# Second products by seven half-size products in all twelve pairs, and a new list of single steps

## The chip, the cores and the metric

The kernel runs on one core of a Trainium2 chip. Its engines are TensorE (PE in the profile, with PEld for its weight loads), the vector engine (DVE), the scalar engine (ACT), GpSimd (POOL, which also issues most of the loads) and SyncE (SP, which issues the stores and the turned tiles). Each takes its own instructions in order, and they wait for each other on semaphores. The metric is the device time of one execution in microseconds. The kernel before takes 168.75 us (median of three runs, 168.35 to 170.79).

## The reference

Two stages. The first is a linear attention with a decaying state, over batch 4, 8 heads, 768 steps, 48 numbers a head:

```
for t in range(S):
    cur = einsum('bhd,bhe->bhde', u * k[t], v[t])
    y[t] = einsum('bhd,bhde->bhe', r[t], state + cur)
    state = w[:, None] * state + einsum('bhd,bhe->bhde', k[t], v[t])
```

The second takes y as 3072 tokens of 384 numbers through two matrices with a leaky gate between, 384 to 2048 and back to 384:

```
h = x @ w_in
g = maximum(0.01 * h, h)
out = g @ w_out
```

Inputs and output are 32-bit floats; the kernel multiplies in bf16 and adds in 32 bits.

## The kernel before

**Chunks and pairs.** The 3072 tokens are 24 chunks of 128 (six for each batch entry). A chunk n goes through these steps, named by the letter that they have in the list ORDER: loads of k, r and v (L213); P scales r and k by powers of the decay (L313); T turns the scaled tile with TensorE for chunks 0 to 7 (L369, evicted by L376), and from chunk 8 on P itself issues a turning DMA on SP (L316); A multiplies keys by queries into two PSUM banks (L389); M masks the scores into the tile `at` (L399 for chunks from 6 on, L407, L423 and L419 before); K multiplies keys by values (L439); S brings the state on (L482 and L484); Q computes the bonus of the same step, for chunks from 6 on by two products and a sum (L343, L345, L347), after which GpSimd writes it on the diagonal of `at` (L355), and the mask fills in the rest; Y multiplies scores by values and state by queries (L512) and is evicted to `xT` (L532).

Two chunks make a pair m of 256 tokens. G (a chunk and a quarter of the hidden units, L545) or J (a pair and an eighth, L562) is the first product of the second stage, evicted through the gate to `gT` (L550, L568). G serves pairs 0 and 1, J the others.

**The second product** has two forms. H takes a chunk: 16 matmuls of 384 columns into one bank (L579), one eviction (L585), a store. Z takes a pair in seven half-size products, the scheme of Strassen and Winograd: the pair's block of 256 tokens by 2048 hidden units is cut into 2 x 2 blocks, `w_out` too. V forms four sums of blocks of `w_out` once (`tw`, L599); B forms four sums of blocks of `gT` for each pair (`gs`, L617); each of seven products is eight matmuls of 192 columns (L651) into one of three banks, with part sums kept by ACT (`snap`, L659) and added by the vector engine (L682). H serves pairs 0 to 7, Z pairs 8 to 11.

**What sets the order.** ORDER is a written list. Each step records its operations, matmuls and evictions together, one engine after another; `Sched` keeps for every tile who wrote and who read it last, and from that puts the waits on each engine's stream. PSUM banks are dealt out in turn by `next_bank`, and `I` in the list skips some. The condition under which an earlier operation on the same engine isn't waited for stands in `Sched.add`:

```
if d.dma is None and d.eng == eng and dma is None and (eng == "pe" or not raw):
    continue
```

so an engine other than TensorE waits for its own earlier operation where it reads what that wrote, and not where it overwrites what that wrote or read.

Of the kernel before, what the change touches and what calls it, by code (L numbers as in the profile page):

```python
# [12 lines left out]
L = 128  # L13
# [10 lines left out]
EARLY = 3  # L24
ORDER = """
v0 U k1 k2 I1 P0 r1 P1.1 r2 k3 T0 F4 C W A0 r3 X0 P2.1 wi3 T1 K0 M0.0 Q0 T2 X1 S0 P3.1 Y0 X2 A2 M2.4 T3 v1 K1 G0.3 k4 Q1 A1 r4 A3 S1 P4 v2 K2 M1.2 T4 v3 k5 Y1 X3 Q2 M3.0 wi2 S2 K3 Y2 Q3 G1.3 G1.2 r5 r6 k6 v4 wi1 G2.2 v5 r7 wi0 v6 Y3 r9 k7 X4 P5 T5 k9 v7 S3 G2.3 P6 T6 Q6 G3.3 K4 A4 X5 G2.1 G0.1 Q4 K5 G1.1 G0.2 M4.4 Q5 A5 S4 M5.2 wo0 wo1 wo2 wo3 A6 Y4 G0.0 G3.1 Y5 M6 P7 G3.2 k8 r8 T7 G3.0 k18 Q7 K6 v10 r12 J2.3 r20 k13 J2.7 v8 r13 r11 S6 k10 J2.2 v20 k11 K7 G1.0 S7 G2.0 J2.6 A7 J2.0 Q9 P9 J2.5 J2.1 M7 J2.4 P8 H1 k12 r21 v9 I4 H0 H2 Y7 Y6 A9 Q8 I1 A8 v21 H3 J3.3 K8 M9 H4 M8 S8 J3.4 J3.7 v13 k20 k14 r10 J3.6 v12 Q13 k16 Y8 k23 Y9 r15 r14 H5 J4.0 J4.3 J3.5 v14 Q11 v23 k15 K9 P12 J4.4 J4.7 J4.5 J4.2 P11 P10 J3.0 I3 Q12 J3.2 P13 I1 S9 P14 K10 J4.6 J4.1 K12 Q10 S10 K13 S12 J3.1 H8 A12 r17 S13 v11 k17 v16 r18 P15 I1 A10 H9 M12 A11 M10 A13 H6 Q15 M11 K14 M13 Y10 I1 v17 k21 Y11 v19 Y12 S14 Y13 P17 r19 Q14 A15 v15 A14 J5.3 v22 J5.7 r16 J5.5 H7 Q17 v18 M15 I4 M14 J5.1 J5.2 J6.4 J6.1 J6.7 J6.2 J6.0 Y14 Q18 I1 P18 Y15 k22 r22 k19 A17 r23 J5.0 K15 J7.5 J7.3 J5.4 S15 P16 I4 J6.3 K16 J6.6 K18 M17 J6.5 Q16 J7.2 P21 S16 J7.0 A18 S18 M18 P19 H13 I1 J7.7 Q20 P20 I2 J5.6 Q21 J7.1 J7.4 K19 J7.6 K20 S19 H10 H12 H11 S20 A20 Q19 A19 A16 H14 M20 H15 M19 M16 A21 Y16 Y17 Y18 I1 V0 V1 M21 Y20 Y19 Y21 J8.1 Q23 J8.0 P23 K21 J8.7 J9.5 P22 S21 J8.6 J9.4 J9.7 K22 J8.5 V2 J8.3 Q22 I2 J9.1 S22 J8.2 J9.2 J8.4 A22 M22 A23 B8.0 M23 B8.2 B8.1 J10.0 J9.3 B8.3 J10.7 J9.6 V3 Z8.0 Y23 Y22 J9.0 B9.0 B9.2 J10.1 B9.1 J10.2 J10.6 I4 Z8.1 J10.3 Z8.2 B9.3 Z8.3 J11.2 Z8.4 Z8.5 I2 J10.5 Z8.6 J10.4 J11.4 B10.2 J11.0 J11.3 J11.6 J11.5 Z9.0 J11.1 Z9.1 B10.0 J11.7 Z9.2 B11.0 Z9.3 Z11.0 Z10.0 B11.1 Z9.4 Z10.1 B11.2 Z9.5 Z9.6 I1 B10.1 Z11.1 Z11.2 B11.3 Z10.2 Z10.3 B10.3 Z11.3 Z11.4 Z11.5 Z10.4 Z11.6 Z10.5 Z10.6
# [7 lines left out]
class Sched:  # L34
# [8 lines left out]
    def add(self, eng, emit, R=(), W=(), dma=None):  # L43
# [73 lines left out]
def bass_rwkv5_eagle__then__act_leaky_relu_kernel(  # L117
# [68 lines left out]
    taken = [0]  # L186

    def next_bank():
        i = taken[0] % 8
        taken[0] += 1  # L190
        return ps[i], ("ps", i)

    def dram(h, offset, pattern):
        return bass.AP(tensor=h.tensor, offset=h.offset + offset, ap=pattern)

# [8 lines left out]
    def load_one(n, which, pace=()):  # L204
# [8 lines left out]
        add("pool", lambda: G.dma_start(dst, src), R=pace, W=[key], dma=f"{which}{n}")  # L213

    def load_two(n, which, pace=()):
        load_one(n, which, pace)
        load_one(n + 1, which, pace)

    def load_pair(n, pace=()):
        for i in (n, n + 1):  # L220
            for which in "krv":
                load_one(i, which, pace)
# [11 lines left out]

    def row(h):
        return dram(h, 0, [[HD, 1], [1, HD]])

    add("sp", lambda: SP.dma_start(w_row[:, :], row(w)), W=["w_row"], dma="w")
    add("act", lambda: A.dma_start(u_row[:, :], row(u)), W=["u_row"], dma="u")
    load_first("r")  # L240
    load_first("k")
    for hh in range(2):
        for name, src, dst in (("wcol", w, wcol), ("ucol", u, ucol)):
            add("sp", lambda src=src, dst=dst, hh=hh: SP.dma_start(
                dst[64 * hh:64 * hh + D, :], dram(src, hh * D, [[1, D], [2 * D, NP], [1, 1]]), allow_slow_non_contiguous=True),
                W=[f"{name}{hh}"], dma=f"{name}{hh}")
    add("act", lambda: A.preload_act_table_set("natural_log_exp_and_others"))
    add("pool", lambda: G.iota(ramp[:, :], pattern=[[1, 128]], base=0, channel_multiplier=-1,  # L248
                               allow_small_or_imprecise_dtypes=True), W=["ramp"])
    add("dve", lambda: V.memset(ones[:, :], 1.0), W=["ones"])  # L250
    add("dve", lambda: V.memset(one_row[:, :], 1.0), W=["one_row"])
    add("dve", lambda: V.memset(one_row16[:, :], 1.0), W=["one_row16"])

    def fill(n):
        i = taken[0] % 8

        def emit():
            for _ in range(n):
                last = PE.matmul(ps[i][:, :], ones[:, 0:128], ones[:, :], start=True, stop=True)
            return last  # L260

        add("pe", emit, R=["ones"], W=[("ps", i), f"fill{n}"])

    def skip(n):
        taken[0] += n

    ps_w, key_w = next_bank()

    def load(name):
        if name[:2] == "wi":  # L270
            load_win(int(name[2:]))
        elif name[:2] == "wo":
            load_wout(int(name[2:]))
        elif name[:2] in ("rr", "kk", "vv"):
            load_two(int(name[2:]), name[0])
        else:
            load_one(int(name[1:]), name[0])

    add("dve", lambda: V.tensor_scalar(kexp[:, :], ramp[:, 0:1], 1.0, float(MID - 1), ALU.mult, ALU.add),
        R=["ramp"], W=["kexp"])  # L280
    add("dve", lambda: V.tensor_scalar(qexp[:, :], ramp[:, 0:1], -1.0, float(-MID), ALU.mult, ALU.add),
        R=["ramp"], W=["qexp"])
    add("dve", lambda: V.tensor_scalar(ident[:, :], ramp[:, :], 0.0, None, ALU.is_equal), R=["ramp"], W=["ident"])
    add("dve", lambda: V.memset(v_sb[:, :, :].rearrange("p n (h e) -> p (n h) e", e=E)[:, :, D:E], 0.0), W=["v0"])
    add("dve", lambda: V.tensor_scalar(mask[:, :], ramp[:, :], 1.0, None, ALU.is_ge), R=["ramp"], W=["mask"])
    for i in range(NQK):
        add("dve", lambda i=i: V.memset(qk[i][:, :, D:E], 0.0), W=[("qk0", i)])
    add("dve", lambda: V.memset(wl[:, :, :], 0.0), W=["wl"])
    add("dve", lambda: V.memset(wu[:, :, :], 0.0), W=["wu"])
    add("act", lambda: A.activation(u_row16[:, :], u_row[:, :], AF.Copy), R=["u_row"], W=["u_row16"])  # L290
    fill(EARLY)
    add("pe", lambda: PE.matmul(ps_w[:, 0:HD], one_row[:, :], w_row[:, :], start=True, stop=True),
        R=["one_row", "w_row"], W=[key_w, "bc"])
    add("act", lambda: A.activation(lnw[:, :], ps_w[:, 0:HD], AF.Ln), R=[key_w], W=["lnw"])
    add("act", lambda: A.activation(qtab[:, :], lnw[:, :], AF.Exp, scale=qexp[:, 0:1]), R=["lnw", "qexp"], W=["qtab"])
    add("act", lambda: A.activation(ktab[:, :], lnw[:, :], AF.Exp, scale=kexp[:, 0:1]), R=["lnw", "kexp"], W=["ktab"])
    at_bank, kv_bank, turns = {}, {}, {"sum": 0, "s": 0}

    def hd(x):
        return x.rearrange("p (h d) -> p h d", d=D)  # L300

    def k_of(n):
        return k_sb[:, n % NRK, :] if n else k0_f[:, :]

    def r_of(n):
        return r_sb[:, n % NRK, :] if n else r0_f[:, :]

    def prep(n, how=0):
        iq = n % NQK
        if n >= 4 or how:  # L310
# [495 lines left out]
```

## Time and profile before

| | us |
|---|---|
| median of the runs | 168.75 |
| the profiled execution | 170.19 |
| its span, first to last instruction | 168.4 |
| TensorE busy | 158.4 (94%) |
| vector engine busy | 112.5 (67%) |
| ACT busy | 94.1 (56%) |
| GpSimd busy | 88.4 (52%) |

A row of the chain of waits gives start, length and the work that the end depended on. A row of a stretch gives its bounds, its length, busy time (and instructions) of PE, PEld, DVE, ACT and POOL, the granted clock (1.00 is full), the share of the DMA engines and GB/s. A row of a group gives line, engine, operation, tiles out<-in with shapes, how many; then busy us and mean ns of one; then the idle time of the engine just before them and what ended it. A timeline row gives start, length and the instruction. A matmul's length there contains its latency; how fast matmuls follow each other is read from the chain.

### The profile page before, as it was taken

Reading aid. Unit: us, or ns where it says so; the run is one execution under the profiler, and the core shown is the slowest. Engines: PE = TensorE matmul, PEld = TensorE weight load, DVE = VectorE, ACT = ScalarE, POOL = GpSimd, SP = SyncE. Lnnn points to the kernel's source line nnn. Section 1 sums busy time; section 2 is a strip of 40 time slices with the busy share of each in tenths; the row PEclk is TensorE's granted clock in tenths of the full one; section 3 lists DMA queues with packets and bytes.
Section 4 is the critical chain, followed back from the end, with each engine's and each line's share of the span. In section 5 each row is a group of like instructions: output and inputs, shape, how many; then the busy total and the mean of one; then the engine's idle time right before and its main releaser. Section 6 shows DMA issues by size and latency. Waiting matters only on the chain.

```text
span 168.4 us, 5024 instructions
## 1 busy us (share of the span) xinstructions
PE 158.4 (94%) x2166; PEld 125.5 (75%) x2166; DVE 112.5 (67%) x205; ACT 94.1 (56%) x179; POOL 88.4 (52%) x101
## 2 busy tenths in 40 slices
PE   6677897999999999999999999999999999999993
PEld 2245796898666778965778886766698889999992
DVE  7398989938405678759896399924899396313571
ACT  4765586787413366841548783521288788385310
POOL 7999999679999199581988732320032000000000
DMA  5999999999999999999999985512126000110224
GB/s 98 120 140 149 166 183 159 194 202 146 139 137 187 178 157 136 183 163 174 129 156 165 128 97 106 125 47 96 48 64 115 0 4 0 47 51 0 77 69 140
DMA packets 100090, 19.67 MB, mean 117 GB/s; under 512 B 93154, under 2 KB 100068, under 8 KB 100068
## 3 DMA queue, kind: packets, MB, share of 16 engines
q0 software_dynamic: 76512, 10.03, 94.2%
q1 hardware_dynamic: 22514, 9.12, 26.2%
q8 instruction: 17, 0.28, 0.7%
q10 hardware_dynamic: 1042, 0.20, 0.6%
q14 instruction: 5, 0.04, 0.1%
HBM read 20.45 MB, written 4.72 MB: 149 GB/s over the span
## 4 chain that ended last, share of the span: by engine, by line
PE 82%; POOL 10%; DMA 6%; issue 1%; ACT 0%; POOLq 0%; ACTq 0%
PE ps_all L562 31%; PE ps_all L579 25%; PE ps_all L651 11%; POOL rk_sb L213 6%; DMA w_in_sb<-in_moe_w_in_dram 6%; PE ps_all L512 5%; PE ps_all L545 4%; PE ps_all L389 3%; POOL v_sb L213 3%; PE ps_all L439 2%; POOL w_in_sb L228 1%; PE ps_all L517 0%; PE ps_all L369 0%; ACT out_sb L675 0%; POOL ramp L248 0%
## 5 line engine op out<-in xcount | busy, mean ns | idle before, releaser
L562 PE MATMUL ps_all<-xT,w_in_sb 128*128 128x256 bf16 x480 | 57.0, 273 | 0.0
L568 ACT ACTIVATE gT<-ps_all 128x512 bf16<-128x512 f32 x80 | 47.8, 597 | 12.3 <-PE ps_all L562 8.7
L562 PEld LDWEIGHTS ps_all<-xT,w_in_sb 128*128 128x128 bf16 x480 | 45.8, 98 | 6.1
L579 PE MATMUL ps_all<-w_out_sb,gT 128*128 128x384 bf16 x256 | 43.5, 326 | 0.0
L355 POOL TENSOR_SCALAR_AFFINE_SELECT at<-s_tok 128x1024 bf16<-128x1024 f32 x18 | 21.0, 1168 | 40.9 <-DVE s_tok L347 40.9
L579 PEld LDWEIGHTS ps_all<-w_out_sb,gT 128*128 128x128 bf16 x256 | 24.4, 98 | 15.8
L399 DVE CAST_PREDICATED at<-mask,ps_all 128x1024 bf16<-128x1024 uint16 x18 | 21.4, 1219 | 18.6 <-PE ps_all L389 18.5
L585 ACT ACTIVATE out_sb<-ps_all 128x384 f32<-128x384 f32 x16 | 7.9, 492 | 37.0 <-PE ps_all L579 37.0
L213 POOL DMA_DIRECT2D v_sb<-in_v_dram x24 | 22.6, 946 | 0.3 <-issue 0.3
L213 POOL DMA_DIRECT2D rk_sb<-in_k_dram x23 | 21.3, 937 | 0.0
L213 POOL DMA_DIRECT2D rk_sb<-in_r_dram x23 | 21.2, 930 | 0.0
L313 DVE TENSOR_TENSOR qk<-rk_sb,tab 128x768 bf16<-128x768 bf16 x23 | 14.5, 638 | 3.9 <-DMA rk_sb<-in_r_dram 3.7
L545 PE MATMUL ps_all<-xT,w_in_sb 128*128 128x128 bf16 x192 | 12.5, 219 | 1.6 <-DMA w_in_sb<-in_moe_w_in_dram 1.1
L482 DVE TENSOR_TENSOR sum_t<-ps_all,st 128x384 bf16<-128x384 f32 x14 | 7.8, 554 | 9.1 <-PE ps_all L439 9.0
L545 PEld LDWEIGHTS ps_all<-xT,w_in_sb 128*128 128x128 bf16 x192 | 11.1, 98 | 2.0 <-ACT gT L550 1.3
L550 ACT ACTIVATE gT<-ps_all 128x512 bf16<-128x512 f32 x16 | 9.6, 603 | 4.6 <-PE ps_all L545 4.2
L532 ACT ACTIVATE xT<-ps_all 128x384 bf16<-128x384 f32 x24 | 10.5, 493 | 2.6 <-PE ps_all L517 2.0
L512 PE MATMUL ps_all<-at,v_sb 128*32 128x128 bf16 x384 | 10.5, 220 | 0.9 <-DVE vs L338 0.9
L512 PEld LDWEIGHTS ps_all<-at,v_sb 128*32 128x32 bf16 x384 | 8.2, 96 | 3.0 <-issue 1.2
L347 DVE TENSOR_REDUCE s_tok<-ku 128x8 f32<-128x384 bf16 x18 | 10.0, 553 | 0.6
L376 ACT ACTIVATE tp<-ps_all 128x512 bf16<-128x512 f32 x16 | 8.6, 602 | 2.7 <-PE ps_all L369 2.7
L617 DVE TENSOR_TENSOR gs<-gT 128x1024 bf16<-128x1024 bf16 x8 | 5.4, 687 | 7.0 <-PE ps_all L651 5.3
(75 smaller groups left out, 185.7 us busy)
## 6 DMA issues: line engine op xcount, KB each, us to landing
out_dram<-out_sb SPq DMA_DIRECT2D x22, 192.0 KB, 2.4
v_sb<-in_v_dram POOLq DMA_DIRECT2D x24, 96.0 KB, 6.5
rk_sb<-in_k_dram POOLq DMA_DIRECT2D x23, 96.0 KB, 6.2
rk_sb<-in_r_dram POOLq DMA_DIRECT2D x23, 96.0 KB, 6.9
w_in_sb<-in_moe_w_in_dram POOLq DMA_DIRECT2D x4, 384.0 KB, 8.2
w_out_sb<-in_moe_w_out_dram POOLq DMA_DIRECT2D x4, 384.0 KB, 10.4
out_dram<-out_sb SPq DMA_DIRECT2D x4, 96.0 KB, 1.6
tp<-qk SPq DMA_TRANSPOSE x16, 4.7
```

The source lines that it names most:

```text
L213: add("pool", lambda: G.dma_start(dst, src), R=pace, W=[key], dma=f"{which}{n}")
L313: add("dve", lambda: V.tensor_tensor(qk[iq][:, :, 0:D], both, by, ALU.mult), R=[("r", n % NRK), ("k", n % NRK), "qtab", "ktab", ("qk0", iq ...
L347: add("dve", lambda: V.tensor_reduce(s_tok[i2][:, :].rearrange("p (two m) -> p two m", two=2), ku[i2][:, :].rearrange("p (m two d) -> p tw ...
L355: add("pool", lambda: G.affine_select(out=at[ia][:, :, :, :].rearrange("p two m i -> p (two m) i"), in_=s_tok[i2][:, :].unsqueeze(2).to_br ...
L399: add("dve", lambda: V.copy_predicated(at[n % NAT][:, :, :, :].rearrange("p two m i -> p (two m) i"), mask[:, :].bitcast(mybir.dt.uint16). ...
L512: last = PE.matmul(ps_y[32 * q:32 * q + 32, 128 * s:128 * s + 128], a, m, start=first_mm and (s == 0 or n >= DIAG), stop=last_mm and n >= ...
L532: add("act", lambda: A.activation(xT[m % NX][:, :, 128 * half:128 * half + 128], ps_y[:, 0:HD].rearrange("p (s t) -> p s t", t=128), AF.Copy),
L545: last = PE.matmul(ps_g[:, 128 * f:128 * f + 128], w_in_sb[:, s, 128 * fb:128 * fb + 128], xT[ix][:, s, t], start=s == 0, stop=s == NSL - 1)
L562: last = PE.matmul(ps_g[:, 256 * f:256 * f + 256], w_in_sb[:, s, 128 * fb:128 * fb + 128], xT[ix][:, s, :], start=s == 0, stop=s == NSL - 1)
L568: add("act", lambda: A.activation(gT[ig][:, 2 * j:2 * j + 2, :].rearrange("p f t -> p (f t)"), ps_g[:, :], AF.Prelu, alpha=0.01), R=[key], ...
L579: last = PE.matmul(ps_o[:, 0:HD], gT[ig][:, s, 128 * half:128 * half + 128], w_out_sb[:, s, :], start=s == 0, stop=s == NFB - 1)
L651: done = PE.matmul(ps_o[:, 0:NH], lhs[:, s, :], rhs[:, s, :], start=first and s == 0, stop=s == HF - 1, skip_group_check=not (first and last))
```

## The change

The second products of all twelve pairs take the form Z; H is in the list no longer. Each step of the list is now one operation of one engine: a matmul step and its eviction, a scaled tile and its turning DMA, the last add of a half and its store are steps of their own (small letters j, g, z, o are the evictions and stores of J, G, Z; C and O those of T and Y; E, f, R, L are the four parts of Q; B and W those of S, b is the sum of gate blocks, t that of `w_out`). A step that opens a PSUM bank names it behind an @. The list is written anew, from the first loads on; the setup that stood ahead of it is in it too, as p0 to p32. The loads of the weights come in the order i1, i0, i3, i2 (before: 3, 2, 1, 0), w2, w3, w0, w1.

```diff
-ORDER = """
-v0 U k1 k2 I1 P0 r1 P1.1 r2 k3 T0 F4 C W A0 r3 X0 P2.1 wi3 T1 K0 M0.0 Q0 T2 X1 S0 ...
-...
-J2.0 Q9 P9 J2.5 J2.1 M7 J2.4 P8 H1 k12 r21 v9 I4 H0 H2 Y7 Y6 A9 Q8 I1 A8 v21 H3 J3.3 K8 M9 H4 M8 S8 ...
+ORDER = """
+p1 p0 p9 p19 q4 p18 p2 r2 q1 p3 q3 p15 p4 p11 p8 q2 p10 p5 p21@0 k2 q0 p14 p13 p12 p17 p6 p16 k1 p7 F1.512.12@1
+...
+G1.2@3 R9 g3.2 w1 V5 G0.2@0 g1.2 L9 M7 G2.3@5 r11 K6@1 b1.0 K7@2 g2.3 Y5@3 O4 B6 v8 G2.2@7 b0.0 O5 k11 Y6@1 b0.1
+...
+Z1.0@7 j3.0 j2.5 Z0.1@4 v10 P11 j2.0 J3.2@1 b1.3 z0.0 v17 j3.3 Z1.1@5 t3 j3.2 r15 Z0.2 j2.7 E11 t2 z1.0 v11
+Z0.3@6 z0.2 z1.1 z0.1 K8@3 b2.0 k14 A9@01 Z0.4 z0.3 M9 L8 Z1.2 Z0.5 v16 B8 z1.2 z0.4 A8@01 W8 Z1.3@6 b2.1 J3.6@3
+M8 Z0.6 E10 Z1.4 P13 j3.6 z0.5 Y8@0 P10 Y9@1 O8 z1.3 X10 Z1.5 z1.4 O9 P12 Z2.0@6 E12 f11 X12 f10 K9@3 J3.4@4
+...
-            if d.dma is None and d.eng == eng and dma is None and (eng == "pe" or not raw):
+            if d.dma is None and d.eng == eng and dma is None and eng == "pe":
                 continue
...
-    def next_bank():
-        i = taken[0] % 8
-        taken[0] += 1
-        return ps[i], ("ps", i)
+    def bank(at=0):
+        where = unit[0].split("@")[1:]
+        return int(where[0][at]) if where else 0
+    def opened(name, at=0):
+        i = bank(at)
+        banks[name] = i, (("ps", i) if "@" in unit[0] else ("ps", name))
+        return banks[name]
...
-    def fill(n):
+    def fill(n, size, which=0):
...
+    def seven(m, k):
+        where, left, right, opens, ends = (FINAL if is_final(m) else INNER)[k]
+        i, key = opened(("Z", m, where)) if opens else banks[("Z", m, where)]
...
+    def taken(m, k):
...
     for name in ORDER.split():
-        if name[0].islower():
-            load(name)
-            continue
-        steps[name[0]](*(int(x) for x in name[1:].split(".") if x))
+        unit[0] = name
+        steps[name[0]](*(int(x) for x in name[1:].split("@")[0].split(".") if x))
```

F is a run of matmuls on ones, whose result nobody reads: two runs of 3 and 4 with 512 columns before, four single ones with 512 and seven with 256 after. In pair 11 the list ends with the adds and four stores of half tiles, as before. The sets SUMS_PE, KU_POOL, ST_POOL and GS_POOL, which would move some steps to other engines, are empty.

More of the change, by code (lines that the diff above doesn't have):

```diff
@@ L281, in bass_rwkv5_eagle__then__act_leaky_relu_kernel @@
[L281 to L287, printed above, removed]
@@ L296, in bass_rwkv5_eagle__then__act_leaky_relu_kernel, with scaled @@
[L296 to L308, printed above, removed]
+        add("pe", emit, R=["ones"], W=[key])
+    def scaled(n, half=None):
         iq = n % NQK
-        if n >= 4 or how:
+        if half is None:
@@ new lines, in crossbar, with turn, emit @@
+    def crossbar(n):
+        iq = n % NQK
+        add("sp", lambda: SP.dma_start_transpose(tp[n % NTP][:, :, :], qk[iq][:, :, :].rearrange("p h e -> p (h e)")),
+            R=[("kp", iq), ("qp", iq), ("qk0", iq)], W=[("tp", n % NTP, 0), ("tp", n % NTP, 1)],
+            dma=f"tp{n % NTP}")
+    def turn(n, half):
+        iq = n % NQK
+        i, key = opened(("T", n, half))
+        def emit():
+            for p in range(NP):
+                h0 = half * H + 2 * p
+                last = PE.matmul(ps[i][:, 128 * p:128 * p + 128],
+                                 qk[iq][:, h0:h0 + 2, :].rearrange("p h e -> p (h e)"), ident[:, :],
+                                 start=True, stop=True)
+            return last
+        add("pe", emit, R=[("kp" if half else "qp", iq), ("qk0", iq), "ident"], W=[key])
@@ L327, in diag, with turned, product @@
+    def turned(n, half):
+        i, key = banks[("T", n, half)]
+        it = n % NTP
+        dst = tp[it][:, NP * half:NP * half + NP, :].rearrange("p m t -> p (m t)")
+        add("act", lambda: A.activation(dst, ps[i][:, :], AF.Copy), R=[key], W=[("tp", it, half)])
+    def product(n):
         it, i2 = n % NTP, n % 4
@@ L379, in a_mm, with scores @@
-    def a_mm(n):
+    def scores(n):
         it = n % NTP
-        if taken[0] % 8 == 7:
-            taken[0] += 1
-        at_bank[n] = (next_bank(), next_bank())
+        one, two = opened(("A", n, 0)), opened(("A", n, 1), 1)
         def emit():
             for p in range(NP):
-                for hh in range(2):
-                    rows = slice(64 * hh, 64 * hh + D)
-                    last = PE.matmul(at_bank[n][hh][0][:, 128 * p:128 * p + 128], tp[it][rows, NP + p, :],
-                                     tp[it][rows, p, :], start=True, stop=True)
-            return last
-        add("pe", emit, R=[("tp", it, 0), ("tp", it, 1)], W=[key for _, key in at_bank[n]])
@@ L506, in emit @@
         def emit():
-            columns = [column(q) for q in range(4)]
+            columns = [column_of(q) for q in range(4)]
             for step in range(max(len(x) for x in columns)):
@@ new lines, in is_final, with emit @@
+    def is_final(m):
+        return m == NST // 2 - 1
+    def seven(m, k):
+        where, left, right, opens, ends = (FINAL if is_final(m) else INNER)[k]
+        i, key = opened(("Z", m, where)) if opens else banks[("Z", m, where)]
+        if isinstance(left, int):
+            lhs, reads = gs[m % 2][left], [("gs", m % 2, left)]
+        else:
+            r, c = left
+            lhs = gT[m % NG][:, HF * c:HF * c + HF, 128 * r:128 * r + 128]
+            reads = [("gT", m % NG, r, j) for j in range(4 * c, 4 * c + 4)]
+        if isinstance(right, int):
+            rhs = tw[right]
+            reads = reads + [("tw", right)]
+        else:
+            rhs = w_out_sb[:, right[0], right[1]]
+            reads = reads + [("wout", j) for j in range(4)]
+        def emit():
+            for s in range(HF):
+                done = PE.matmul(ps[i][:, 0:NH], lhs[:, s, :], rhs[:, s, :], start=bool(opens) and s == 0,
+                                 stop=s == HF - 1, skip_group_check=not (opens and ends))
+            return done
+        add("pe", emit, R=reads + ([("seven", m, k - 1)] if k else []), W=[key, ("seven", m, k)])
```

622 lines of the change are left out of this document (309 added, 313 removed).

## The prediction

> **What bounds the kernel now.** I read the page first, then the chain of waits in order of time, then busy time by stretch, then the groups of the two engines that the change loads and unloads.
>
> ```profile
> span 168.4 us, 5024 instructions
> PE 158.4 (94%) x2166; PEld 125.5 (75%) x2166; DVE 112.5 (67%) x205; ACT 94.1 (56%) x179; POOL 88.4 (52%) x101
> PE   6677897999999999999999999999999999999993
> ```
>
> TensorE (PE) is full from the tenth of 40 slices on to the last but one; the vector engine (DVE) is two thirds busy. The chain, start and length in us:
>
> ```profile
> by line: PE ps_all L562 31.5%; PE ps_all L579 25.1%; PE ps_all L651 11.0%; POOL rk_sb L213 5.9%; DMA w_in_sb<-in_moe_w_in_dram 5.5%; PE ps_all L512 5.0%; PE ps_all L545 4.1%; PE ps_all L389 3.2%; POOL v_sb L213 2.7%; PE ps_all L439 1.5%; PO
> ...
> 17.89 9.31 DMA w_in_sb<-in_moe_w_in_dram
> 27.20 0.14 issue
> 27.34 1.50 PE ps_all L545 x24
> ...
> 34.77 0.45 PE ps_all L369 x8
> 35.22 0.67 PE ps_all L545 x12
> 35.89 0.17 PE ps_all L439 x4
> ...
> 43.24 7.80 PE ps_all L579 x48
> ...
> 51.77 0.55 PE ps_all L389 x16
> 52.33 2.71 PE ps_all L579 x16
> ...
> 60.42 0.90 PE ps_all L512 x56
> ...
> 129.09 3.93 PE ps_all L562 x36
> ...
> 140.59 0.66 PE ps_all L651 x8
> ...
> 153.07 12.55 PE ps_all L651 x152
> 165.62 0.02 issue
> ...
> 165.71 0.33 ACT out_sb L675
> ```
>
> Three parts. A head of 27.3 us ends when a piece of the first weight matrix lands. From 27.34 to 165.62, 138.28 us, TensorE works almost without a gap. A tail of 168.4 - 165.6 = 2.8 us evicts and stores the last half tile. So the end moves by what changes in the head, in TensorE's work behind it, and in new waits inside it.
>
> ```profile
> 0.00:27.30 27.30, 20.32 (x332) 14.05 (x332) 21.75 (x52) 17.86 (x35) 26.32 (x35) 1.00 1.89 145
> 27.30:65.00 37.70, 37.51 (x525) 28.74 (x526) 22.70 (x41) 20.28 (x38) 31.64 (x37) 1.00 2.09 164
> 65.00:105.00 40.00, 40.00 (x522) 31.16 (x520) 30.84 (x53) 23.50 (x43) 25.16 (x27) 1.00 1.54 145
> 105.00:165.60 60.60, 60.60 (x793) 51.56 (x790) 37.16 (x62) 32.12 (x64) 5.28 (x5) 1.00 0.19 54
> ```
>
> By stretch (length, then PE, weight loads, DVE, ACT, POOL), the vector engine works 22.7 + 30.8 + 37.2 = 90.7 us behind the head and has 47.6 us free; the granted clock is 1.00 throughout.
>
> **The second products, TensorE.** Eight pairs now take two L579 steps of 16 matmuls of 384 columns each. The chain gives them 25.1% of 168.4 = 42.3 us for 256 matmuls (2.60 to 2.71 a step: 48 in 7.80, 16 in 2.71). They become seven products of eight matmuls of 192 columns a pair, 8 x 56 = 448. The four pairs that have this form show 152 in 12.55 us, 82.6 ns each, and a lone product between other work costs the same, eight in 0.66. 448 x 82.6 ns = 37.0. TensorE is freed of 42.3 - 37.0 = **5.3 us**, all on the path.
>
> **The second products, the other engines.**
>
> ```profile
> L617 DVE TENSOR_TENSOR gs<-gT 128x1024 bf16<-128x1024 bf16 x8 | 5.4, 687 | 7.0 <-PE ps_all L651 5.3 <-ACT gT L568 1.6
> L682 DVE TENSOR_TENSOR out_sb<-ps_all,snap 128x192 f32<-128x192 f32 x13 | 4.6, 357 | 5.5 <-PE ps_all L651 5.5
> L659 ACT ACTIVATE snap<-ps_all 128x192 f32<-128x192 f32 x12 | 4.0, 331 | 4.9 <-PE ps_all L651 4.6
> L585 ACT ACTIVATE out_sb<-ps_all 128x384 f32<-128x384 f32 x16 | 7.9, 492 | 37.0 <-PE ps_all L579 37.0
> ```
>
> The vector engine gains 8 x 4 sums of gate blocks at 0.687 and 8 x 3 adds at 0.357: 22.0 + 8.6 = 30.6 us, so 143 busy us in some 164. ACT loses 16 evictions at 0.492 and gains 8 x 4 at 0.331, +2.7 us; it is 56% busy and I cost it at nothing (2.7 if its slack were gone). So the free 47.6 us of the vector engine shrink to 17, and what matters is where they lie.
>
> **Does the vector engine stay ahead?** I add both engines' instructions along the new list, at the durations shown: a turn 0.45, G 0.67, K 0.17, A 0.28 to 0.30, Y 0.45, J 0.655, Z 0.66. For the vector engine each row less 0.08, because neighbours overlap:
>
> ```profile
> 38.90 0.36 DVE L484 TENSOR_TENSOR st<-sum_t,wl 128x384 bf16<-128x384 bf16 x1
> 39.17 0.35 DVE L343 TENSOR_TENSOR ku<-rk_sb,u_tab 128x384 bf16<-128x384 bf16 x1
> 39.55 0.36 DVE L345 TENSOR_TENSOR ku<-rk_sb,ku 128x384 bf16<-128x384 bf16 x1
> 39.95 0.55 DVE L347 TENSOR_REDUCE s_tok<-ku 128x8 f32<-128x384 bf16 x1
> 40.42 0.55 DVE L313 TENSOR_TENSOR qk<-rk_sb,tab 128x768 bf16<-128x768 bf16 x1
> L399 DVE CAST_PREDICATED at<-mask,ps_all 128x1024 bf16<-128x1024 uint16 x18 | 21.4, 1219 | 18.6 <-PE ps_all L389 18.5
> ```
>
> L343 follows an instruction it doesn't need after 0.27; L345 needs L343 and comes 0.38 after it. The old order has such needy neighbours in every chunk (two L343-L345-L347 steps, one L482-L484), the new one sets other work between nearly all: up to 18 x 2 + 14 steps by 0.11 = 5.5 us less. Against that the recorder now also makes an engine wait for its own earlier reads and writes; the vector engine has 34 waits more in the program (245 against 211), at most 34 x 0.11 = 3.7. I take the gain in the sums, and 0 for the waits, whose partners are mostly many instructions back.
>
> The sums, from the top of the list: before Y6 TensorE has 27.6, the vector engine 28.6; before Y8 45.7 and 44.1; before Z3.0 58.4 and 55.5; later the gap grows past 3. TensorE's clock starts later: it has done 16.7 of its sum when it needs w_in piece 0, at about 26.5, so it runs 9.8 behind its sum. The vector engine is held by the scores of chunk 6: A6 stands at 22.8 of TensorE's sum, so at 32.6 us, its mask (L399, 1.22) ends at about 33.9, and there the vector sum is 25.1: it runs 9 behind its own. So its lead is about 0 at Y6, 2.4 at Y8, 3.7 at Z3.0. Around Y8 and Z3.0 that lead isn't usable in full: two chunks' scores and masks alternate there (A9, M9, A8, M8, Y8; then A10, M10, A12, M12, A11, M11, A13), each mask waits for the score, and the next score for the bank. I take **+1.0 us** of waits, between 0 (the order holds) and 5 (below).
>
> **The head.** In the old order 17 loads and 2 weight pieces were issued ahead of the piece of 17.89 that landed at 27.20. In the new list the deciding piece, w_in 0, is issued behind 18 loads and 1 piece, at much the same time (GpSimd issues without a break there, 26.32 of 27.30 us), with one 384 KB piece less before it and one 96 KB load more: it lands between 25 and 27.2. The turns of chunks 4 and 7, which wait for their loads, let TensorE arrive at about 26. I take a start at 26.5, bounds 25.5 and 28.5 (pieces 3 and 2 come 1 and 5 issues later and could be late in their turn). What is done by then differs: two turns and one A more (1.2 us), three G and a K less (2.2), so 1.0 us more is left. Start 0.8 earlier, 1.0 more left: +0.2 us. The matmuls on ones that keep TensorE awake (7 of 512 columns become 4 of 512 and 7 of 256) lie in this head; without cover they cost under 1 us. They matter if TensorE is cold at 26; the old trace ran on at full speed after a 1.1 us gap, at 0.67 a G.
>
> **Queues.** Stores and turned tiles get steps of their own on SP, POOL's loads stand behind tiles that wait for the vector engine (w_out 0 and 1 behind the tile of chunk 7, the loads of chunks 10 to 13 behind that of 9). Y10 needs v10 some 20 us after its issue, K13 needs v13 about 9 after; that is the closest, against the 9.31 of the slowest piece above. I cost them at nothing; if the cover goes, K13 waits 1 or 2 us. A pair holds three banks for some 10 us where an L579 step held one for 2.6; the list names the banks, and the next user of a bank comes 1 us or more after its eviction in the sums. Nothing, up to 1.
>
> **Sum.** -5.3 + 0.2 + 1.0 = -4.1 us: span 164.3. The profiled execution took 170.19, 1.8 around its span, and would be 166.1; the median of the runs is 168.75, and less 4.1 it is **164.6**, 2.4% faster. 2% (165.4 to 172.1) is about what a measurement can tell from no change.
>
> **Rivals.** (1) *The vector engine becomes the bound in chunks 6 to 15.* For it: the lead of 0 at Y6. Against it: 17 us free in all, and chunks 16 to 23 lie behind a lead of 3 and more. It gives 2 to 5 us of waits in place of 1: 165.5 to 168.6, no change. (2) *GpSimd's tiles stop the vector engine*, the one that ends slower:
>
> ```profile
> 57.15 0.36 DVE L345 TENSOR_TENSOR ku<-rk_sb,ku 128x384 bf16<-128x384 bf16 x1
> 58.23 1.09 POOL L355 TENSOR_SCALAR_AFFINE_SELECT at<-s_tok 128x1024 bf16<-128x1024 f32 x1 [3.60 <-DVE s_tok L347]
> 58.39 1.14 DVE L345 TENSOR_TENSOR ku<-rk_sb,ku 128x384 bf16<-128x384 bf16 x1
> L313 DVE TENSOR_TENSOR qk<-rk_sb,tab 128x768 bf16<-128x768 bf16 x23 | 14.5, 638 | 3.9 <-DMA rk_sb<-in_r_dram 3.7 <-DMA rk_sb<-in_k_dram 0.2
> L345 DVE TENSOR_TENSOR ku<-rk_sb,ku 128x384 bf16<-128x384 bf16 x18 | 8.0, 444 | 0.6
> L343 DVE TENSOR_TENSOR ku<-rk_sb,u_tab 128x384 bf16<-128x384 bf16 x18 | 7.8, 435 | 0.0
> L484 DVE TENSOR_TENSOR st<-sum_t,wl 128x384 bf16<-128x384 bf16 x14 | 6.9, 494 | 0.5
> ```
>
> The same L345 takes 0.36 alone and 1.14 when a tile is being built beside it: it ends with the tile. Against their undisturbed rows (0.55, 0.36, 0.35, 0.36) the four groups lost 2.0 + 1.5 + 1.5 + 1.9 = 6.9 us over 18 tiles, 0.38 a tile. The 32 new gate sums are of this kind, so more tiles will hit one. Ten tiles (chunks 6 to 15) are built while the lead is short; at a full 1.1 us each they cost 11, less the 2.4 of lead at Y8, 8.6 of waits in place of 1.0: 172.2, slower. It decides from about 1.1 us a tile; I expect 0.5. The Trainium skill ("SBUF — State Buffer", section "SBUF: two separate sides") says that the port pair which the vector engine and GpSimd share is an exclusive lock held for a whole instruction, so that the loser stops altogether; by that, every tile that meets a gate sum would cost its full length and the sum would be this rival's. The trace agrees on the single collision (1.14 against 0.36) and not on its frequency (0.38 a tile). (3) *The head comes out otherwise*: weights at 28.5, +2.0: 166.6; or at 25.5, -1.0: 163.6. (4) *The halves don't run at 82.6 ns among other work*: the lone product of 0.66 speaks against it; at 90 ns, 3.3 us are lost, 167.9.
>
> **How the numbers follow.** Forecast 0.53; rival 1 0.24; rival 2 0.08; a late head 0.05, an early one 0.05; rival 4 0.05. Faster by over 2%: 0.53 + 0.05, less 0.03 for the upper edge of the forecast (165.4 is only 0.8 above it): 0.55. Slower: 0.08. Within 2%: 0.37. The range leaves out rival 2, the top of rival 1 and under 1 in 10 below: 162.4 (no waits and the early head, 162.6) to 168.3.
>
> **What would show it.** Right: the chain is TensorE from about 26.5 to 161.5, seven products at 82 to 83 ns, DVE near 140 busy us, TensorE's waits 1 us in all, at masks or banks of chunks 6 to 13. Wrong: TensorE's row of tenths with eights and sevens between 35 and 80 us, waits on gs or at (rival 1); gs with a mean of 0.8 and more (rival 2); a wait for w_in past 28 us (3); L765 over 0.66 a product (4).

## The result, and the profile after

The changed kernel takes 168.17 us (median of 20 runs, 166.94 to 168.98) against 169.06 of the kernel before (20 runs, 168.25 to 172.27). The ratio is 0.9949, 95% interval 0.9924 to 0.9974: half a per cent faster, where the prediction had 2.4%. The profiled executions took 170.19 before and 168.21 after, 2.0 us apart, and not the 4.1 of the sum. The time lies just inside the range that the prediction gave (162.4 to 168.3), at the end where it had put its first rival; that rival's mechanism isn't what happened, so this is luck.

First the page and the chain of waits after (start, length, work):

```profile
span 166.4 us, 5494 instructions
PE 156.9 (94%) x2362; PEld 138.9 (83%) x2362; DVE 129.0 (78%) x261; ACT 88.5 (53%) x195; POOL 89.7 (54%) x101
PE   4598999997999999999999999999999999999993
```

```profile
25.82 0.67 PE ps_all L634 x12
26.51 2.85 PE ps_all L634 x48
...
33.17 1.21 DVE at L497
...
35.62 0.84 PE ps_all L634 x12
...
38.92 0.91 issue
...
40.12 6.66 PE ps_all L656 x60
...
54.97 0.77 PE ps_all L757 x8
...
144.49 3.96 PE ps_all L757 x48
...
153.70 9.91 PE ps_all L757 x120
```

L634 is a G, L656 a J, L757 a half-size product, L601 a Y, L497 a mask. The chain is TensorE as forecast, from 26.5 to 163.6 instead of 161.5, and 120 matmuls in 9.91 are 82.6 ns each. In the row of tenths only one slice behind the fourth is below the others: the tenth, at 37 to 42 us. The chain shows two things there that the prediction didn't have: a mask that TensorE hangs on at 33.17, and 0.91 us of "issue", time in which TensorE waits for nothing that the profile shows, in the middle of the matmuls of Y7.

Then the stretches (bounds, length, then busy us of PE, weight loads, DVE, ACT, POOL) and two groups of the vector engine:

```profile
27.30:65.00 37.70, 36.40 (x593) 33.12 (x591) 33.07 (x63) 20.70 (x45) 26.88 (x31) 1.00 1.86 158
65.00:105.00 40.00, 39.91 (x605) 35.31 (x603) 35.58 (x67) 21.76 (x49) 30.36 (x32) 1.00 1.57 145
```

```profile
L726 DVE TENSOR_TENSOR gs<-gT 128x1024 bf16<-128x1024 bf16 x24 | 17.8, 745 | 15.6 <-ACT gT L665 8.4 <-PE ps_all L757 7.0
L434 DVE TENSOR_TENSOR ku<-rk_sb,u_tab 128x384 bf16<-128x384 bf16 x18 | 7.1, 400 | 0.0
L439 DVE TENSOR_TENSOR ku<-rk_sb,ku 128x384 bf16<-128x384 bf16 x18 | 6.9, 399 | 0.1
```

Against the rows of before TensorE has lost 1.1 us of busy time between 27 and 65 us and 0.1 between 65 and 105. The vector engine is at 33 and 36 us where it was at 23 and 31, without stopping TensorE. So the waits are all early, ahead of 40 us.

### The profile page after: what moved, and what is told of

The parts are those of the page before. It is cut to its first block, busy times and chain, and to the rows that moved or that the text cites. A ratio compares the mean times of both kernels' runs of the same rounds, so it can differ in the third digit from the quotient of the medians.

```text
span 166.4 us, 5494 instructions
## 1 busy us (share of the span) xinstructions
PE 156.9 (94%) x2362; PEld 138.9 (83%) x2362; DVE 129.0 (78%) x261; ACT 88.5 (53%) x195; POOL 89.7 (54%) x101
## 4 chain that ended last, share of the span: by engine, by line
PE 77%; DVE 11%; issue 3%; DMA 3%; ACT 2%; POOL 2%; DVEq 0%; POOLq 0%
PE ps_all L757 30%; PE ps_all L656 28%; PE ps_all L601 5%; PE ps_all L634 4%; PE ps_all L473 4%; DMA rk_sb<-in_r_dram 3%; DVE gs L726 2%; PE ps_all L413 2%; POOL rk_sb L274 2%; PE ps_all L531 2%; DVE ku L434 2%; DVE s_tok L444 1%; DVE at L497 1%; DVE qk L391 1%; ACT tp L424 1%
## 5 line engine op out<-in xcount | busy, mean ns | idle before, releaser
L665 ACT ACTIVATE gT<-ps_all 128x512 bf16<-128x512 f32 x80 | 44.8, 604 | 31.9 <-PE ps_all L656 28.6
L656 PE MATMUL ps_all<-xT,w_in_sb 128*128 128x256 bf16 x480 | 58.9, 273 | 0.1
L656 PEld LDWEIGHTS ps_all<-xT,w_in_sb 128*128 128x128 bf16 x480 | 45.5, 98 | 5.7 <-DVE out_sb L778 0.3
L726 DVE TENSOR_TENSOR gs<-gT 128x1024 bf16<-128x1024 bf16 x24 | 17.8, 745 | 15.6 <-ACT gT L665 8.4
L757 PE MATMUL ps_all<-tw,gs 128*128 128x192 bf16 x288 | 28.9, 246 | 0.0
L497 DVE CAST_PREDICATED at<-mask,ps_all 128x1024 bf16<-128x1024 uint16 x18 | 21.7, 1219 | 6.6 <-PE ps_all L473 6.2
L757 PEld LDWEIGHTS ps_all<-tw,gs 128*128 128x128 bf16 x288 | 24.0, 98 | 0.7
L757 PE MATMUL ps_all<-w_out_sb,gT 128*128 128x192 bf16 x192 | 19.5, 246 | 0.0
L768 ACT ACTIVATE snap<-ps_all 128x192 f32<-128x192 f32 x36 | 11.3, 341 | 11.9 <-PE ps_all L757 11.8
L757 PEld LDWEIGHTS ps_all<-w_out_sb,gT 128*128 128x128 bf16 x192 | 16.1, 98 | 0.6
L778 DVE TENSOR_TENSOR out_sb<-ps_all,snap 128x192 f32<-128x192 f32 x37 | 12.4, 351 | 2.9 <-PE ps_all L757 2.7
L391 DVE TENSOR_TENSOR qk<-rk_sb,tab 128x768 bf16<-128x768 bf16 x23 | 12.6, 550 | 2.2 <-DMA rk_sb<-in_r_dram 1.2
L634 PE MATMUL ps_all<-xT,w_in_sb 128*128 128x128 bf16 x192 | 12.4, 219 | 0.4 <-issue 0.2
L634 PEld LDWEIGHTS ps_all<-xT,w_in_sb 128*128 128x128 bf16 x192 | 11.0, 98 | 1.0 <-issue 0.4
L601 PE MATMUL ps_all<-at,v_sb 128*32 128x128 bf16 x384 | 10.7, 220 | 0.9 <-issue 0.9
L644 ACT ACTIVATE gT<-ps_all 128x512 bf16<-128x512 f32 x16 | 8.8, 603 | 4.6 <-PE ps_all L634 4.6
```

The lines of the kernel that those rows point to most:

```text
L391: add("dve", lambda: V.tensor_tensor(qk[iq][:, :, 0:D], both, by, ALU.mult), R=[("r", n % NRK), ("k", n % NRK), "qtab", "ktab", ("qk0", iq ...
L497: add("dve", lambda: V.copy_predicated(dst, mask[:, :].bitcast(mybir.dt.uint16).unsqueeze(1).to_broadcast([128, H, 128]), raw), R=keys + [ ...
L601: last = PE.matmul(ps_y[32 * q:32 * q + 32, 128 * s:128 * s + 128], a, m, start=first_mm and (s == 0 or whole), stop=last_mm and whole)
L634: last = PE.matmul(ps[i][:, 128 * f:128 * f + 128], w_in_sb[:, s, 128 * fb:128 * fb + 128], xT[ix][:, s, t], start=s == 0, stop=s == NSL - 1)
L656: last = PE.matmul(ps[i][:, 256 * f:256 * f + 256], w_in_sb[:, s, 128 * fb:128 * fb + 128], xT[ix][:, s, :], start=s == 0, stop=s == NSL - 1)
L665: add("act", lambda: A.activation(gT[ig][:, 2 * j:2 * j + 2, :].rearrange("p f t -> p (f t)"), ps[i][:, :], AF.Prelu, alpha=0.01), R=[key] ...
```

## The experiments

The kernel before and the changed kernel once more, for second traces, in one group:

> The kernel before, unchanged, for a second trace. The profiled execution that the prediction started from took 170.19 us, but the median of 20 runs is 169.06 and eleven of the 20 lie between 168.25 and 169.3. Theory: executions of the kernel before differ in when the first weights land, so a trace near 168.5 us has its dense TensorE stretch starting 1.2 to 1.7 us ahead of 27.34 us and the same length behind it (138.3, give or take 0.3). Rival: it differs by waits inside the dense stretch; then the stretch starts at 27.3 again and is shorter.

> The changed kernel, unchanged, as the control of this group and for a second trace. Expected 168.2 us, 0.995 of the kernel before. If the waits of TensorE between 32 and 40 us (2.3 us in the first trace, a pause of 0.91 in the middle of the Y step of chunk 7 among them) belong to the program they come again at the same steps; if they are chance they are elsewhere or gone, with the time some 1 us lower in such an execution.

The first gave 170.06 (8 runs, ratio 1.004, 0.9991 to 1.0089), its profiled execution 169.29; 23 other runs of the same kernel in that group have a median of 168.99, so the median of a few runs of it can move by a microsecond, as much as most effects below; the second 168.37 (12 runs, ratio 0.9945, 0.9915 to 0.9975), its profiled execution 167.89. From the chain of the first:

```profile
20.85 1.62 PE ps_all L545 x26
...
26.09 1.58 PE ps_all L545 x24
...
42.23 7.80 PE ps_all L579 x48
...
152.22 12.55 PE ps_all L651 x152
```

The dense work starts at 26.09 where the first trace of before has 27.34, and the first three full products at 42.23 against 43.24; from there to the last row the two take 110.0 and 109.8 (152.22 - 42.23 and 153.07 - 43.24). TensorE's wait for w_in, 1.1 us in the first trace, isn't in the second. So these two executions differ ahead of 42 us, by when the weights land, as the theory had it; the stretch from 26.09 to the end (164.77) is 138.7, 0.4 more than 138.28 and a little outside the 0.3 expected. The execution that the prediction started from was a late one: 170.19 where the median is 169.06. So 0.9 (against the second trace) to 1.1 us (against the median) of the 2.0 between the profiled executions come from the one before being late.

The second trace of the changed kernel shows the pause of Y7 again, at the same matmul: it belongs to the program. Which matmul it is shows in the stretches that end at the pause, by the number of matmuls (after PE's busy time) that were begun. For the changed kernel, then its second trace, then the kernel before and its second trace:

```profile
0.00:38.80 38.80, 33.12 (x600) 25.82 (x600) 32.31 (x72) 24.58 (x48) 35.14 (x45) 1.00 1.85 151
```

```profile
0.00:39.60 39.60, 32.24 (x600) 24.78 (x600) 33.61 (x74) 24.57 (x48) 35.88 (x46) 1.00 1.87 153
```

```profile
0.00:20.95 20.95, 15.09 (x219) 9.27 (x219) 16.04 (x43) 12.64 (x25) 19.97 (x28) 1.00 1.90 134
0.00:33.40 33.40, 26.32 (x472) 19.49 (x473) 27.13 (x61) 22.24 (x43) 31.35 (x41) 1.00 1.90 150
```

```profile
0.00:20.80 20.80, 15.35 (x219) 9.51 (x219) 15.98 (x43) 12.64 (x25) 19.83 (x28) 1.00 1.89 134
0.00:32.40 32.40, 26.66 (x472) 19.75 (x473) 26.15 (x61) 22.41 (x43) 31.38 (x41) 1.00 1.91 149
```

Read off the start of every matmul, the gaps of over 0.3 us up to 42 us stand ahead of these ordinals (start of the matmul behind it, and distance from the one before it; the ends of a step's own wait left out):

```
after         472 (33.81, 0.46)  600 (39.84, 1.13)
after, again  345 (28.02, 0.86)  600 (39.66, 0.85)
before        219 (20.96, 0.70)  472 (33.48, 0.37)
before, again 219 (20.85, 0.67)  472 (32.46, 0.52)
packets of the queue "q8 instruction", 16 KB each, after:  18.7  25.1  31.4  37.5  42.9  53.5 ...
```

Two programs with different orders stop at ordinals of one series, 126 to 128 apart, and all but one of the four traces at 472. That is the supply of instructions: 128 matmuls with 128 weight loads are 256 instructions, and the page's row of that queue has 18 transfers and 0.29 MB, 16 KB each, 64 bytes an instruction (before: 17 transfers; 2 x 2362 and 2 x 2166 instructions by 256 are 18.5 and 16.9). The Trainium skill ("Runtime: NRT & Kernel Launch", section "Instruction fetch mechanics") says that an engine's instruction memory is refilled in blocks of 16 KiB, 256 instructions, the next one while the current one runs, and that crossing a block is mostly hidden; the trace agrees on the block, and in the first 42 us not on the hiding: 0.9 us here. Until 40 us a new piece comes every 6.1 to 6.4 us. Steps of small matmuls go through one faster than that: a Y has 28 in 0.45 us, where a J has 6 in 0.66.

The packets of this queue tie the two together. Each pause in the list ends 1.3 to 1.6 us after a piece has landed (after: a piece from 37.52 to 38.49, TensorE goes on at 39.84; before: 18.57 to 19.54, and 20.96). And the pieces follow TensorE: in the eleven traces compared, the fourth piece, for which the 600th matmul waits where there is a pause, begins 2.6 to 3.7 us after TensorE has passed the 472nd (33.81 to 37.52 after) and takes about 1.0. So TensorE gets from the 472nd to the 600th in about 6 us when the piece is the limit (33.81 to 39.84, and 33.64 to 39.66 in the second trace).

Four experiments on this pause. The first moves Y7 behind two J steps of six long matmuls:

```diff
-Y6@1 b0.1 Y7@6 k10 E8 J2.5@5 O7 B7 g2.2 J2.3@6 P9 k13 g0.2 b1.2 X9 J2.4@7 O6 k12 W7 j2.3 J2.1@0 f8 P8 r13 J2.0@6
+Y6@1 b0.1 k10 E8 J2.5@5 B7 g2.2 J2.3@6 P9 k13 g0.2 Y7@0 b1.2 X9 O7 J2.4@7 O6 k12 W7 j2.3 J2.1@6 f8 P8 r13 J2.0@0
```

> The changed kernel with one step moved: the output product of chunk 7 (56 small matmuls) stands behind two steps of six long matmuls more, with another bank. The traces of the changed kernel show TensorE standing still at the 131st, the 472nd and the 600th matmul, 128 apart at the end, and 128 matmuls with their weight loads are 256 instructions, 16 KB at 64 bytes: one of the 18 pieces of 0.29 MB on the instruction queue. Supply theory: the pause of 0.9 us in the middle of this step is the wait for the next piece, which comes at 39.8 us whatever TensorE does; with 12 long matmuls (1.3 us) in place of small ones ahead of the 600th, TensorE gets there at about 40 and the pause is gone: 0.7 to 0.9 us faster than the changed kernel, 167.3 us. Rival, that the step waits for something of its own (its tile, its values): the pause moves with the step or the time stays, 168.2.

(Y7 has 28 matmuls, not the 56 of this text; the pause comes after 22 of them.) 168.46 (12 runs, ratio 0.9955, 0.993 to 0.998): no gain. But the chain shows no pause in Y7 and another wait behind it:

```profile
38.61 1.42 PE ps_all L656 x12
...
40.58 0.87 ACT xT L619 x2
...
42.00 4.76 PE ps_all L656 x42
```

ACT evicts in order, and j2.3 now stands behind O7 and O6: J2.1 waits 0.71 us for the bank of J2.3, which it takes over in this edit. The edit made that wait itself. With j2.3 ahead of O7:

```diff
-g0.2 Y7@0 b1.2 X9 O7 J2.4@7 O6 k12 W7 j2.3 J2.1@6
+g0.2 Y7@0 b1.2 X9 j2.3 O7 J2.4@7 O6 k12 W7 J2.1@6
```

> As the kernel with the output product of chunk 7 behind two long steps, but with the eviction of the second of them ahead of that of the product, so that the scalar engine's order makes no new wait (the 0.71 us at 42.00, for a gate, of the first try). Supply theory: no pause at the 600th matmul and none behind it, 0.7 to 0.9 us faster than the changed kernel: 167.4. Rival, that the time is set elsewhere: 168.2 again.

167.52 (6 runs, ratio 0.9916, 0.9886 to 0.9945), 0.65 under the changed kernel's median, though the intervals overlap (0.9924 to 0.9974 there). There is no pause at the 600th matmul and none behind it, and the trace bears the gain out: the 727th matmul starts at 51.22, where the two traces of the changed kernel have 51.93 and 51.76. The other edit takes up the mask at 33.17. In the timeline after, a gate sum of pair 0 runs beside GpSimd's tile for chunk 7 and ends with a delay:

```profile
31.56 1.14 POOL L459 TENSOR_SCALAR_AFFINE_SELECT at<-s_tok 128x1024 bf16<-128x1024 f32 x1 [1.69 <-DVE s_tok L444]
31.67 1.57 DVE L726 TENSOR_TENSOR gs<-gT 128x1024 bf16<-128x1024 bf16 x1
33.17 1.21 DVE L497 CAST_PREDICATED at<-mask,ps_all 128x1024 bf16<-128x1024 uint16 x1
...
36.62 0.68 DVE L726 TENSOR_TENSOR gs<-gT 128x1024 bf16<-128x1024 bf16 x1
```

1.57 against 0.68. The edit, first alone and then with Y7 moved:

```diff
-L7 A7@67 b0.2 A6@01 g1.3 Y4@4 M6 K5@5 G3.2@2 w0 W4 G1.2@3 R9 g3.2 w1 V5 G0.2@0 g1.2 L9 M7 G2.3@5
+L7 A7@67 A6@01 g1.3 Y4@4 M6 K5@5 G3.2@2 w0 W4 G1.2@3 R9 g3.2 w1 V5 G0.2@0 g1.2 L9 M7 b0.2 G2.3@5
```

> The changed kernel with one gate sum of pair 0, which ran beside GpSimd's tile of chunk 7 (1.57 us in place of 0.68) and held up the mask of chunk 6, moved behind the mask of chunk 7. Theory of the vector engine's hold-up: the mask of chunk 6 ends some 0.9 us earlier, the waits of 0.4 and 0.3 us behind it at 32 to 35 us go, and the time falls by 0.5 to 0.7, to 167.6. Supply theory: the waits go, but the pause at the 600th matmul grows by as much, because the instructions come no earlier: 0 to -0.2, 168.1.

> The same with the gate sum of pair 0 behind the mask of chunk 7. Alone that gained nothing, and the pause at the 600th matmul grew from 0.9 to 1.3 us. Supply theory: with room ahead of the 600th matmul the 0.4 to 0.5 us of it show now: 167.0, a gain that is larger than the sum of the two edits alone. Rival, that the gate sum is worth nothing: 167.4, as without it.

Alone: 168.62 (12 runs, ratio 0.9965, 0.9933 to 0.9998), no gain, and its timeline says why: the mask starts 1.06 earlier, TensorE comes to the 600th matmul 0.8 earlier (38.12), and the pause grows from 0.91 to 1.32:

```profile
32.11 1.22 DVE L497 CAST_PREDICATED at<-mask,ps_all 128x1024 bf16<-128x1024 uint16 x1 [0.55 <-PE ps_all L473]
...
39.44 0.23 PE L601 MATMUL ps_all<-at,v_sb 128*32 128x128 bf16 x2 [1.32 <-issue]
```

Both: 167.13 (6 runs, ratio 0.9894, 0.9861 to 0.9926), 1.0 under the changed kernel, the best of all kernels here. The gate sum gains nothing alone; with the pause gone the medians differ by 0.4, but the intervals of e13 and e14 overlap and in the traces the 727th matmul starts only 0.14 earlier (51.08), so its worth there isn't settled. That the pause is a matter of supply doesn't hang on it: a wait of Y7's own would have moved with Y7, and not grown when the mask came earlier. In the run with the gate sum moved alone TensorE passes the 472nd matmul at 33.3 and goes on with the 600th at 39.4, again 6.1 later: a wait removed between two such ordinals comes back at the second. Two pauses are left in this kernel's trace, 0.71 ahead of matmul 345 and 0.46 ahead of 472. (The changed kernel and this one were timed in different groups; their intervals touch at 0.993.)

The changed kernel without its F steps:

> The changed kernel without its eleven matmuls on ones (they write nothing that is read). Work theory: they stand where TensorE waits anyway, and leaving them out changes nothing, or costs up to 1 us where TensorE then runs colder in the head (the granted clock of the first 27 us tells). Supply theory: every matmul less ahead of the 600th brings the following ones forward by a 128th of the 6 us that a piece of instructions takes, 11 x 47 ns = 0.5 us: 167.7.

168.38 (12 runs, ratio 0.9949, 0.9915 to 0.9983). The half microsecond that supply promised isn't there, and single runs spread from 167.58 to 170.59 where the changed kernel's second group lies between 167.89 and 168.79. Its profiled execution (169.48) pauses ahead of matmul 219 like before, and shows one more thing, in the chain:

```profile
19.55 1.39 PE ps_all L634 x12
```

A G of 12 matmuls takes 0.67 elsewhere: TensorE is at half its pace there. The 1.00 that the views print as granted clock for this stretch isn't a measurement, since this trace holds no record of the clock (nor does the first trace of before, where the prediction read 1.00 throughout). The pace can be read from the matmuls of 128 columns: they follow each other every 107 ns up to 22.7 us here and every 56 ns from 23.7. In the first trace of the changed kernel that change lies between 14.4 and 15.0, and its first clock record, 1.00, begins at 14.65; in the first trace of before it lies at 10.2, so the prediction's rows behind the head are at full pace. The Trainium skill ("TensorE: Matmul & The Clock Gate", section "Part 1: The HAM clock gate") has TensorE at half rate until it has been busy for a few microseconds; the row agrees with the half rate, and how long TensorE must be busy isn't shown here. So the run settles nothing about supply (its first five pieces come late as well, 1.5 to 3.6 us behind those of the changed kernel's first trace), but in this one execution it shows what the F steps are for.

The vector engine with more to do. Two of four gate sums are made twice in pairs 2 to 7:

```diff
-Z0.3@6 ... b2.0 ... b2.2 ...
+Z0.3@6 ... b2.0 b2.0 ... b2.2 b2.2 ...
```

> The changed kernel with two of the four gate sums made twice for pairs 2 to 7: 12 instructions of some 0.65 us, 7.8 us more for the vector engine between 38 and 105 us, the output unchanged. This doubles the suspected load. The prediction's first rival, a vector engine that becomes the bound in chunks 6 to 15: 4 to 7 us slower, 172 to 175. Theory, that from 40 us on the vector engine is ahead with some 12 us of slack in 40 to 105 us: 0 to 1.5 us slower, 168.2 to 169.7.

177.05 (4 runs, ratio 1.047, 1.0421 to 1.052), 8.9 over the changed kernel. My theory of 12 us of slack falls. Its page, and stretches of it and of the changed kernel:

```profile
PE 157.7 (90%) x2362; PEld 138.3 (79%) x2362; DVE 138.1 (79%) x273; ACT 88.8 (51%) x195; POOL 90.9 (52%) x101
```

```profile
40.00:70.00 30.00, 28.47 (x372) 25.68 (x364) 25.70 (x51) 16.06 (x36) 21.17 (x24) 1.00 1.65 127
70.00:130.00 60.00, 54.30 (x830) 47.83 (x827) 56.43 (x106) 29.05 (x65) 33.13 (x33) 1.00 1.15 116
```

```profile
40.00:70.00 30.00, 30.00 (x390) 27.01 (x385) 25.47 (x49) 16.66 (x37) 20.83 (x23) 1.00 1.92 144
70.00:130.00 60.00, 59.91 (x954) 54.05 (x953) 52.61 (x102) 32.46 (x73) 32.55 (x33) 1.00 1.11 121
```

12 instructions, 9.1 us more of the vector engine (138.1 - 129.0), and 8.9 us more of the kernel. In the profiled execution 1.5 of them lie ahead of 42 us, where the two lists are the same: all three pauses are there, and the 600th matmul starts at 41.30 instead of 39.84. The last matmul starts 9.2 later, so 7.7 belong to the edit. In the changed kernel the vector engine is idle for 4.5 and 7.4 us of these stretches; that idle time isn't spare, since it lies ahead of masks and gate sums that wait for TensorE and ACT (in the group's row of gs: 15.6, put down to gT and to products), and an engine that works in order can't use it for what stands behind.

Last, the products and the order one without the other. The changed order with full products in pairs 0 to 7, placed at two of the seven products' places; then the old order with seven products in a row and their sums behind the pair's last gate (first forms of both compute something else; they took 188.35 and 206.35. The forms below store each product at once, and use banks that hold nothing else):

```diff
 (the changed order, without b0.0 to b7.3)
-Z2.1@4 j3.7 M10 o0 ... z2.1 b2.2 ... Z2.5 ... z2.5
+H4@6 j3.7 M10 ... h4 o4 ... H5@4 ... h5 o5
```

> The changed order, but pairs 0 to 7 make their second products the old way: two full products of 16 matmuls of 384 columns, at the places of two of the pair's seven half-size products, each stored at once, without those pairs' 32 gate sums. This separates the products from the order. As the prediction had it, 5.3 us more of TensorE: 173.5 us. Theory after the traces: 16 products at 2.60 against 56 at 0.66 are 41.6 - 37.0 = 4.6 us more, less what the missing sums free between 32 and 40 us (0 to 0.5, since the pause for instructions takes it back): 172.3 to 172.8. Rival, that the 30 us added to the vector engine ate the gain: TensorE's waits vanish and the time stays within 170.

```diff
 (the old order, V0 to V3 ahead of the first product)
-G1.0 S7 G2.0 ... H1 ... H0 H2
+G1.0 B0.0 B0.1 B0.2 B0.3 S7 G2.0 B1.0 ... Z0.0 Z0.1 Z0.2 Z0.3 Z0.4 Z0.5 Z0.6 ...
```

> The old order and the old waits, but pairs 0 to 7 make the seven half-size products, all seven in a row at the place of the pair's later full product, in banks that hold nothing else at that place; the gate sums stand right behind the pair's last gate block, the four weight sums ahead of the first product. This does the products without the order. Theory: 4.6 us of TensorE come off before's 169.1 and 1 to 4 us come back as waits, since the old order leaves the vector engine no room: 165.5 to 168.5. Rival, that the new order is what makes the products possible at all: waits of 5 us and more, 169.5 to 175.

185.97 (6 runs, ratio 1.0968, 1.0899 to 1.1037) and 205.55 (4 runs, ratio 1.2153, 1.2093 to 1.2212). Both expectations fail: either half of the change alone, placed as here, is 16.5 or 36.2 us slower than the kernel before in the same group. In the second, the chain from 37 to 54 us goes through sums, one after the other, with TensorE standing:

```profile
37.84 0.61 ACT gT L569
38.47 0.70 DVE gs L636
39.20 1.90 DVE gs L636 x3
41.09 0.48 DVE sum_t L501
41.95 0.61 DVE gs L636
42.66 0.76 DVE gs L636 x2
...
47.87 0.88 DVE tw L618
48.88 5.42 PE ps_all L673 x48
```

The last of these rows is 113 ns a matmul and not 82.6: the granted clock is 0.50 from 48.2 to 51.5 us and 0.931 over the span. So a part of the 36 us is a slower TensorE, 14 us of clock at most by an estimate from these two numbers (0.069 x 202.5).

In the first, the full products read all of a pair's gates until their end, and the gates of a later pair, which the new order wants early, wait for them (8.2 us in two places); the chain then goes through these gates, the evictions behind them on ACT and the product that needs the bank:

```profile
52.91 2.06 ACT gT L660 x4
54.98 0.78 ACT out_sb L680 x2
55.80 2.77 PE ps_all L671 x16
```

So neither run gives the price of the products as a difference of times, and that was their aim. Their steps give it: 16 matmuls in 2.60 and 2.71 to 2.77 there, eight in 0.66 and 0.77 after. These two placements are mine, and a better one of either half wasn't tried.

## Why the prediction was wrong

The forecast for the median was 164.6, 3.6 below the 168.17 measured: 2.1 in the span (166.4 instead of 164.3), and 1.4 in the base, because the sum took a span from an execution of 170.19 and subtracted its gain from a median of 168.75. In the span the step that failed in kind is the term of the waits; the products and the work left at the start were mis-sized.

**Bound.** Right: TensorE, from the head to the end, without a stop of more than a quarter of a microsecond behind 40 us.

**The products, 5.3 us: mis-sized.** 42.3 us came from the chain's share of L579, 2.64 a step. But a step takes 2.60, and 2.71 only behind one with small matmuls; that 0.11 doesn't go with the old products. After, it falls on others (54.97: a product of 0.77 instead of 0.66). 16 x 2.60 - 56 x 0.66 = 41.6 - 37.0 = 4.6, so 0.7 too much. The 82.6 ns, which rival 4 doubted, hold (at L757, the L765 of the text).

**Work left at the start, 1.0: mis-sized.** "Two turns and one A more 1.2" took 0.45 a turn from a row of eight matmuls. A turn step has four: 0.22. So 1.45 were left. **The start** was put at 26.5 and came 0.85 earlier: G2.0, the first step that needs piece 0, begins at 25.65 by the start of its first matmul (the chain has it from 25.82), TensorE's one wait for a transfer is that of 2.3 us for the row of w at the very start, and a late or early head (rival 3) didn't decide.

**Waits, 1.0: the step that failed in kind.** By the steps' times over their usual ones TensorE loses 2.5 us, about 2.2 of it between 32 and 40 us: 0.9 in the one pause, 0.4 ahead of the 472nd matmul (33.81), the rest around the late mask. The place was foreseen roughly (no lead at Y6) and the cause wasn't: the sums had TensorE and the vector engine as the only clocks, and a third ran beside them, the instructions. The old order went through the same 600 matmuls by 42.4 us, 4.5 after the piece for the next had landed (37.97); the new one by 38.8, 0.3 after, and went on 1.0 later. The gate sum's delay (0.89 in one collision) is rival 2's mechanism, once; what it costs when the supply is out of the way is 0.1 to 0.4 by the trace and the medians.

The sum: 0.7 + 0.45 + 1.5 - 0.85 = 1.8 of the 2.1 us by which the span of 166.4 exceeds the 164.3 forecast; 0.3 stay unassigned. And of the 2.0 us that the two profiled executions do differ, about 1 comes from the one before being late in its head. Working from the median with the span of one late execution (170.19 against 168.75, a difference that the text named) hid that a part of the 27.34 us of head, 1.1 of waiting for w_in, isn't in every run.

**Rival 1** (vector engine the bound in chunks 6 to 15) is off as stated: TensorE isn't stopped by it from 40 us on. But "17 us free in all" was no argument against it: 9.1 us more cost 8.9, or 7.7 without the head. The forecast of a lead that "grows past 3" counted idle time as lead. **Rival 2** is off: gs at a mean of 0.745 in the row shown (0.72 over all 48), and ku at 400 and 399 ns where it had 435 and 444, so the collisions haven't become more expensive as a whole. **143 busy us** became 129: neighbours overlap more than was taken, and collisions cost less. **ACT and queues at nothing**: right; no wait for a load or an eviction behind 40 us.

## What to carry to other kernels

Count instructions as well as microseconds: where a dense engine goes through 256 instructions faster than a piece of them arrives (6 us here in the first 42), moving small steps behind long ones was worth more (some 0.6 us) than speeding up what feeds them (nothing that shows), and a wait removed between two such points came back at the second. Idle time of an engine that works in order is slack only if later work could be pulled into it; doubling a few of its instructions tells. And take the base of a sum from an execution near the median, or say which part of the span the executions differ in.

## What the runs showed of the hardware

- TensorE pauses for instructions at fixed ordinals (219, 345, 472, 600), for 0.2 to 1.3 us, in the first 42 us alone, and goes on 1.3 to 1.6 us after a piece of 16 KB has landed. They show as "issue" of TensorE, never as a wait for something, and they grow when the work ahead of them gets shorter. Later the distance alone isn't the limit: after, TensorE goes from the 1236th matmul to the 1363rd in 3.9 us (86.86 to 90.72) without a pause, and the piece had landed 3.2 us before. Why a piece starts only some 3 us behind TensorE in the head wasn't tried: the traffic of the loads is one candidate, but the row of the DMA engines stays at 9 tenths far behind 40 us, where no pause is left.
- In the run without the F steps TensorE ran at half pace until 23 us (a G of 12 matmuls in 1.39), in a trace without any record of the clock, for which the views print 1.00. The spacing of equal matmuls (107 against 56 ns) told the pace where the record was missing.
